# A chunk-selecting attention with a gated linear unit: one fp16 maximum for the bound's operands, and another order of the steps

## The chip, the cores and the metric

One core of one Trainium2 chip runs the whole program, one launch. Its TensorE (PE) multiplies, VectorE (DVE), ScalarE (ACT) and GpSimd (POOL) do the rest, and the queue of SyncE (SP) issues most transfers. The metric is the device time in microseconds of one execution.

## The reference

Batch 4, 8 heads, 768 positions, 64 dimensions, in float32. Keys are cut into 24 chunks of 32. For every query an upper bound of its score with each chunk is computed from the chunk's smallest and largest key values. The six causal chunks with the largest bounds are kept, and attention runs over these alone. Its output goes through a causal convolution of five taps, a sigmoid, a product with a value projection and an output projection.

```python
k_min, k_max = np.min(k_chunks, axis=3), np.max(k_chunks, axis=3)
ub = np.sum(np.maximum(q[:, :, :, None, :] * k_min[:, :, None, :, :],
                       q[:, :, :, None, :] * k_max[:, :, None, :, :]), axis=-1)
ub = np.where(causal, ub, -1000000000.0)
top_chunks = np.argsort(ub, axis=-1)[..., -6:]
scores = scale * np.matmul(q, k.transpose(0, 1, 3, 2))
scores = np.where(sel & causal_positions, scores, -1000000000.0)
attn = softmax(scores) @ v                       # then x = heads side by side, 512 wide
gate = 1.0 / (1.0 + np.exp(-causal_conv5(x, conv_w)))
return (gate * (x @ w_val)) @ w_out
```

## The kernel before

The work is 16 pairs of heads (four to a batch). A pair's two heads lie side by side on the 128 partitions. The kernel is a graph of named steps (`build`, inner function `pair`). They are emitted in an order written out by hand in `ORDER` (some 1,600 names), and each engine runs its own steps in that order. A step's name has the pair p behind it. Costs given with the steps (`cost`, `lat`, `dma`) are not used when the program is emitted.

- **Loads** `Lk`, `Lq`, `Lv`: keys, queries and values of a pair by SP's queue, into four buffers each. Pair 0 loads keys and queries in halves.
- **Transposes** `KT`, `QT` (PE, L649; L640 for pair 0) put keys and queries with the dimension on the partitions, in two PSUM banks of 384 columns each.
- **Evictions** `KE`, `QH` (ACT, L655, L692) write them as fp16; `QH` is 16 q.
- **Chunk extremes** `KX` (DVE, L661): four reductions a pair, maximum and minimum of two halves.
- **Bound operands.** With d = max - min, the bound is relu(q) d + q min. It is computed in fp16 with a high and a low part of each factor. `KB0` to `KB4` and `KS` (POOL, L671 to L688) make the parts of d and min. On DVE, from PSUM, for 640 of the 768 queries and in a 256 and a 384 wide piece: `QL` (L731) is the low part of q, `RH` (L746) relu of 16 q, `RL` (L753) the low part of the relu, as (q > 0) QL. For pair 2 `RH` is on ACT. Pair 0 goes another way: `KF`, `QF`, `RF` (ACT) make fp32 operands, and `BF` (PE, L723) multiplies in fp32.
- **Bounds** `CF` and `BD` (PE, L777, L788; six matmuls for each of five query tiles), **top eight** `T8` (DVE, L796), **compare** `CM` (DVE, L803) with the sixth largest. `MT` and `ME` (PE, then DVE, L817) transpose the mask; for six late pairs a transposing DMA `MD` does it.
- **Scores** `S` (PE, L831 to L836), in six PSUM banks per head: keys times queries, plus a penalty matmul of the mask (`EM`, `QM`). The 192 first query columns need no mask, so a piece that begins there is cut in two matmuls.
- **exp** `E` (ACT, L840; 12 a pair, ten of 512 columns), causal cut `A` on the diagonal (POOL, L852; 8 a pair), values as fp16 `VC` (POOL, L763).
- **Attention times values** `AV` (PE, L861), `RC` and `NR` (DVE) normalise, `XT`, `XTE` transpose (PE and DVE, L904; DMA for seven pairs), `XH` (POOL) copies what the convolution needs across tiles.
- **Convolution** `CV` (PE, L925; two halves of 80 matmuls for every second pair), `TH` (ACT) the gate as a tanh; **value projection** `VL` (PE, L940), `GV` (DVE, L946) gate times value; **output** `OU` (PE, L954), `OE` eviction (ACT, three on DVE), `ST` store (SP).
- **Spare matmuls** `F`, `G` (PE, L972): 36 matmuls whose result nobody reads.

PSUM has eight banks; a step that opens a group takes the bank that has been free longest. Weights (`wval`, `wout`) are loaded by POOL's queue, `wvd` copies a half of them by SP's.

Of the kernel before, what the change touches and what calls it, by code (L numbers as in the profile page):

```python
# [28 lines left out]
class Graph:
# [44 lines left out]
def emit_in_order(graph, names, nbanks=8):  # L74

    at = {o.name: o for o in graph.ops}
    order = [at[n] for n in names]
# [19 lines left out]
    "dmat": set(range(8, 15)),
    "dmam": set(range(10, 16)),
    "xeng": "DVE",
    "cvcost": 1750.0,  # L100
    "split": {0},
    "lq": {},
    "fine": {0},
    "vceng": "POOL",
    "f32": {0},
    "rha": {2},
    "rqeng": "ACT",
# [1012 lines left out]
```

## Time and profile before

| | us |
|---|---|
| runs | 188.33, 189.61, 313.72 (median 189.61) |
| span of the profiled execution | 185.7 |
| PE, DVE, ACT, POOL busy | 173.7, 133.2, 141.9, 103.6 |

The profile is of one execution, from its first to its last instruction; its own run time is not among the data, and the runs above lie 2.6 us and more over its span. A row of a group gives line, engine, operation, what is written and read, the shape and the count; then the busy time, the mean duration in ns, and the idle time of the engine just before, with what ended it. A row of the chain gives start, length and what ran. A step is found by its line.

### The profile page before, as it was taken

What the parts mean: (1) busy time and instruction counts of PE and PEld (TensorE: products, weight loads), DVE (VectorE), ACT (ScalarE), POOL (GpSimd) and SP (SyncE); (2) the same over time, 40 slices, a digit from 0 to 9 for tenths busy, and PEclk for the clock granted to TensorE, in tenths of its full rate; (3) what the DMA queues carried; (4) which work ended last, traced back from release to release, by engine and by line L of the source; (5) the groups of instructions that cost most, each with busy time, mean ns of one, the idle gap of its engine ahead of it and who ended that gap; (6) DMA issues with size and microseconds to landing.
All of it is one profiled execution on the core that took longest, in us unless ns stands there. A gap on an engine that the chain in (4) does not pass through costs nothing.

```text
span 185.7 us, 9267 instructions
## 1 busy us (share of the span) xinstructions
PE 173.7 (94%) x3894; PEld 120.0 (65%) x3894; DVE 133.2 (72%) x457; ACT 141.9 (76%) x322; POOL 103.6 (56%) x294
## 2 busy tenths in 40 slices
PE   7798889999999699999999899999999999999991
PEld 5685657675767576776767678675576646765550
DVE  0588899999999999999998798789425222710541
ACT  2656999999999789999898976837766999162341
POOL 8628789979295997589945408805850363100000
PEclk9999999999999999999999999999999999999999
DMA  4999999999999996099955748919938920017346
GB/s 104 212 220 195 220 178 234 200 196 185 213 176 227 210 195 88 4 203 201 197 106 124 158 91 164 115 35 230 241 101 219 209 95 4 13 38 287 115 167 229
DMA packets 89913, 29.70 MB, mean 160 GB/s; under 512 B 85387, under 2 KB 86667, under 8 KB 89872
## 3 DMA queue, kind: packets, MB, share of 16 engines
q1 hardware_dynamic: 88880, 28.06, 72.0%
q0 software_dynamic: 992, 1.06, 3.9%
q8 instruction: 30, 0.49, 1.1%
q14 instruction: 11, 0.09, 0.2%
HBM read 20.98 MB, written 6.29 MB: 147 GB/s over the span
## 4 chain that ended last, share of the span: by engine, by line
PE 64%; ACT 14%; POOL 6%; DVE 6%; issue 3%; DMA 2%; SPq 2%; DVEq 0%; POOLq 0%; ACTq 0%
PE ps L940 12%; PE ps L954 11%; ACT P L840 11%; PE ps L861 8%; PE ps L925 8%; PE ps L833 6%; PE ps L836 5%; PE ps L649 5%; PE ps L788 4%; DMA kn<-in_k_dram 2%; DVE KK L661 2%; POOL P L852 2%; POOL VA L763 2%; SPq L631 2%; ACT QH L692 1%
## 5 line engine op out<-in xcount | busy, mean ns | idle before, releaser
L840 ACT ACTIVATE P<-ps 128x512 f16<-128x512 f32 (+1 forms) x192 | 90.6, 574 | 7.7 <-PE ps L836 7.3
L852 POOL TENSOR_SCALAR_AFFINE_SELECT P<-P 128x128 f16<-128x128 f16 (+1 forms) x128 | 42.4, 356 | 24.0 <-ACT P L840 22.5
L661 DVE TENSOR_REDUCE KK<-ps 128x12 f32<-128x384 f32 x64 | 32.7, 549 | 8.7 <-PE ps L640 4.2
L836 PE MATMUL ps<-QM,EM 64*128 64x512 f16 (+4 forms) x256 | 37.5, 290 | 0.6 <-DVE QM L817 0.6
L833 PE MATMUL ps<-QH,KE 64*128 64x512 f16 (+4 forms) x256 | 35.4, 291 | 1.5 <-issue 0.8
L946 DVE SCALAR_TENSOR_TENSOR GV<-G,ps 128x384 f16<-128x384 f32 x32 | 16.4, 549 | 23.0 <-PE ps L940 23.0
L861 PE MATMUL ps<-VA,P 128*128 128x65 f16 x672 | 28.9, 194 | 0.0
L861 PEld LDWEIGHTS <-P 128*128 128x128 f16 x672 | 24.1, 98 | 6.5 <-issue 4.3
L962 ACT ACTIVATE OSB<-ps 128x512 f32<-128x512 f32 (+1 forms) x22 | 12.9, 603 | 16.1 <-PE ps L954 10.2
L940 PE MATMUL ps<-xT,wv 64*128 64x384 f16 x256 | 23.2, 323 | 0.0
L954 PE MATMUL ps<-wo,GV 128*128 128x512 f16 (+1 forms) x100 | 22.7, 371 | 0.0
L655 ACT ACTIVATE KE<-ps 128x384 f16<-128x384 f32 x32 | 15.7, 515 | 6.6 <-DVE KK L661 6.1
L796 DVE MAX8 TOP<-ps 128x8 f32<-128x16 f32 (+4 forms) x160 | 15.7, 166 | 4.3 <-PE ps L788 3.9
L930 ACT ACTIVATE G<-ps 128x384 f32<-128x384 f32 x32 | 13.8, 498 | 6.3 <-PE ps L925 6.3
L833 PEld LDWEIGHTS <-KE 64*128 64x128 f16 x256 | 13.6, 94 | 7.6 <-issue 3.3
L940 PEld LDWEIGHTS <-wv 64*128 64x128 f16 x256 | 12.9, 94 | 8.4 <-issue 1.4
L925 PE MATMUL ps<-xT,diag 32*32 32x384 f16 x1280 | 17.6, 326 | 0.0
L871 DVE TENSOR_TENSOR ON<-ps,RCP 128x384 f16<-128x384 f32 x32 | 17.1, 548 | 0.2
L692 ACT ACTIVATE QH<-ps 128x384 f16<-128x384 f32 x32 | 15.1, 507 | 2.1 <-PE ps L649 1.9
L925 PEld LDWEIGHTS <-diag 32*32 32x32 f16 x1280 | 14.1, 88 | 4.0 <-issue 1.6
L763 POOL CAST VA<-vn 128x768 f16<-128x768 f32 x16 | 14.3, 892 | 2.1 <-DMA vn<-in_v_dram 1.8
L836 PEld LDWEIGHTS <-EM 64*128 64x128 f16 x256 | 12.0, 94 | 4.9 <-issue 3.3
(80 smaller groups left out, 302.1 us busy)
## 6 DMA issues: line engine op xcount, KB each, us to landing
vn<-in_v_dram SPq DMA_DIRECT2D x16, 384.0 KB, 5.4
out_dram<-OSB SPq DMA_DIRECT2D x23, 256.0 KB, 2.9
kn<-in_k_dram SPq DMA_DIRECT2D x30, 192.0 KB, 4.5
qn<-in_q_dram SPq DMA_DIRECT2D x30, 192.0 KB, 4.5
wo<-in_moe_w_out_dram POOLq DMA_DIRECT2D x4, 128.0 KB, 3.8
wv<-in_moe_w_val_dram POOLq DMA_DIRECT2D x8, 64.0 KB, 3.3
wv<-wv SPq DMA_DIRECT2D x4, 128.0 KB, 5.0
kn<-in_k_dram SPq DMA_DIRECT2D x4, 96.0 KB, 2.4
```

The source lines that it names most:

```text
L661: nc.vector.tensor_reduce(out=KK[p % 2][:, mx, w * 12:(w + 1) * 12], in_=bank(gr, None).rearrange("p (c t) -> p c t", t=CH), axis=AX.X, op ...
L692: nc.scalar.activation(out=QH[p % 3][:, w * HB:(w + 1) * HB], in_=bank(gr, None), func=AF.Copy, scale=QS)
L763: nc.gpsimd.tensor_copy(out=o, in_=i)
L833: nc.tensor.matmul(out=pq[hh][:, col + a:col + n], lhsT=KE[p % 3][HP[hh], ks], rhs=QH[p % 3][HP[hh], q0 + a:q0 + n], start=True, stop=False)
L836: nc.tensor.matmul(out=pq[hh][:, col + a:col + n], lhsT=EM[HP[hh], ks], rhs=qm[HP[hh], q0 + a - 128:q0 + n - 128], start=False, stop=True)
L840: e.EX = lambda p, hh, bi, tot, gr: nc.scalar.activation(out=PT[hh, bi, p % 2][:, 0:tot], in_=bank(gr, None)[:, 0:tot], func=AF.Exp, scale ...
L852: nc.gpsimd.affine_select(out=ap, in_=ap, pattern=[[0, n], [1, 128]], compare_op=ALU.is_ge, fill=0.0, base=0, channel_multiplier=-1)
L861: nc.tensor.matmul(out=pav[:, qt, :], lhsT=PT[a, bi, p % 2][:, col:col + 128], rhs=VA[p % 3][:, hh, jt, :], start=(jt == 0), stop=(jt == qt))
L871: e.NR = lambda p, hh, gr: nc.vector.tensor_tensor(out=ON[(p // 2) % 2][:, 2 * (p % 2) + hh].rearrange("p t h d -> p h t d"), in0=bank(gr, ...
L925: nc.tensor.matmul(out=pc[i][os], lhsT=diag[rs, cp * NG + gi, j, :], rhs=x[rs, gi, :, a:a + 128], start=(j == 0), stop=(j == 2 * KSZ - 1), ...
L940: nc.tensor.matmul(out=pv[h], lhsT=wval_sb[HP[h], n, wc:wc + 255:2], rhs=xT[HP[h], (b % 2) * 2 + cp, gi, :, LD:LD + 128], start=(n == 0), ...
L954: nc.tensor.matmul(out=po[:, 0:z - a], lhsT=GVT[(b % 2) * NCT + et][:, s * 128:(s + 1) * 128], rhs=wout_sb[:, et, a:z], start=(et == 0), s ...
```

## The change

- `RH` and `RL` are replaced by one step `RR`: maximum with 0 of the high and the low part of q together, 2 x 640 columns of fp16 from SBUF to SBUF, on DVE. For that `QL` lies beside `QH` in one tile, and `QH` is rounded down a little in its scale (16 (1 - 2^-11)), so that the low part has the sign of q.
- Pair 0 goes the fp16 way like the others, and its loads are whole. `KF`, `QF`, `RF`, `BF` go.
- The parts of d and min are made in six steps `KB0` to `KB5` without an intermediate tile.
- An unmasked piece of the scores is no longer cut in two matmuls; 64 matmuls fewer, the same columns.
- The table `alt` gives 71 steps another engine than the usual one: to DVE 14 `KE`, 13 `QH`, 19 `OE`, 14 `KB`, two `XH` and one `VC`; to ACT five `ME`, two `XTE`, one `KB`.
- 43 spare matmuls in five groups.
- `ORDER` is another order of the steps, with the PSUM bank of each group written behind an @.

```diff
 PARAMS = {
-    "kbeng": ["POOL", "POOL", "POOL"],
     "border": [5, 3, 4, 2, 1, 0],
...
+    "alt": dict(w.split(":") for w in """
+KB0.1:ACT ME0:ACT KE2.1:DVE KE3.0:DVE QH4.0:DVE XTE0:ACT ME3:ACT KE5.1:DVE QH5.1:DVE ME4:ACT
+QH6.0:DVE KB6.2:DVE KB6.5:DVE KE7.0:DVE QH7.1:DVE KE8.0:DVE KB7.5:DVE QH8.1:DVE KB7.2:DVE
...
+OE3.5z:DVE OE3.5:DVE OE3.0:DVE OE3.3:DVE OE3.2:DVE OE3.1:DVE
...
 ORDER = """
+mfz em0 em1 ident mKB0 Lk0 F0@2 F1 F2 F3 F4 F5 F6 F7 F8 F9 F10 F11 F12 F13 KT0@01 KX0.11 KX0.00
+cfill mNS0 identh ident2 identb KE0.1 mVA2 mKB1 Lq0 em2 KX0.10 Lk1 G0@4 G1 G2 G3 G4 G5 G6 G7 G8 G9
+G10 QT0@23 H0@1 H1 H2 H3 H4 H5 H6 H7 H8 H9 H10 KT1@45 KX0.01 Lq1 QH0.0 Lk2 Lq2 Lk3 Lq3 QL0.0 QH0.1
+KB0.0 KB0.1 KB0.2 KE0.0 KE1.0 KB0.3 Lv0 Lk4 KB0.5 QL0.1 KB0.4 mVA0 RR0 KX1.10 KX1.11 CF0@6 CF1@7
...
-QS = 16.0
+QR = 16.0
+QS = QR * (1.0 - 2.0 ** -11)
...
-            g.op(eng, cr, lr, f"RH{p}.{w}", lambda w=w, gr=gr, eng=eng: e.RHv(p, w, gr, eng),
-                 [("Q", "ps", p, w)], [("RH", k2, w)], [gr])
...
-            g.op("DVE", c, l, f"RL{p}.{w}", lambda w=w, gr=gr: e.RLv(p, w, gr),
-                 [("Q", "ps", p, w), ("QL", k2, w)], [("RL", k2, w)], [gr])
...
+        eop("DVE", f"RR{p}", lambda eng: e.RRv(p, eng),
+            [("QH", k3, w) for w in range(2)] + [("QL", k3, w) for w in range(2)], [("RR", k2)])
...
-    RH = [ct_([128, SELT * 128], F16, f"RH{i}") for i in range(2)]
-    RL = [ct_([128, SELT * 128], F16, f"RL{i}") for i in range(2)]
+    QQ = [ct_([128, 2, S], F16, f"QQ{i}") for i in range(3)]
+    QH = [t[:, 0] for t in QQ]
+    RR = [ct_([128, 2, SELT * 128], F16, f"RR{i}") for i in range(2)]
...
+    def scaled(eng, out, in_, f):
+        if eng == "ACT":
+            nc.scalar.activation(out=out, in_=in_, func=AF.Copy, scale=f)
+        elif f == 1.0:
+            (nc.vector if eng == "DVE" else nc.gpsimd).tensor_copy(out=out, in_=in_)
+        else:
+            (nc.vector if eng == "DVE" else nc.gpsimd).tensor_scalar(
+                out=out, in0=in_, scalar1=f, scalar2=None, op0=ALU.mult)
...
+        hh = n % 2
+        o, i = kb[HP[hh], :, CC[hh] * NCH:(CC[hh] + 1) * NCH], kk[HP[hh]]
+        if n < 4:
+            scaled(eng, o[:, 0:2], i, 1.0)
         else:
...
+            en.tensor_tensor(out=o[:, 2:4], in0=i, in1=o[:, 0:2], op=ALU.subtract)
...
+    def RRv(p, eng):
+        (nc.vector if eng == "DVE" else nc.gpsimd).tensor_scalar(
+            out=RR[p % 2], in0=QQ[p % 3][:, :, 128:S], scalar1=0.0, scalar2=None, op0=ALU.max)
...
-                if a:
-                    nc.tensor.matmul(out=pq[hh][:, col:col + a], lhsT=KE[p % 3][HP[hh], ks],
-                                     rhs=QH[p % 3][HP[hh], q0:q0 + a], start=True, stop=True)
-                nc.tensor.matmul(out=pq[hh][:, col + a:col + n], lhsT=KE[p % 3][HP[hh], ks],
-                                 rhs=QH[p % 3][HP[hh], q0 + a:q0 + n], start=True, stop=False)
+                nc.tensor.matmul(out=pq[hh][:, col:col + n], lhsT=KE[p % 3][HP[hh], ks],
+                                 rhs=QH[p % 3][HP[hh], q0:q0 + n], start=True, stop=False,
+                                 skip_group_check=True)
```

Up to the step `CV3.0` the two orders hold the following numbers of steps on DVE and ACT (before, after). DVE: `KX` 52, 52; `RH` 22, 0; `RL` 24, 0; `QL` 24, 26; `RR` 0, 12; `KE` 0, 9; `QH` 0, 8; `ME` 10, 5; `XTE` 8, 6; `KB` 0, 5; `T8` 60, 60; `NR` 19, 19. ACT: `E` 132, 128; `KE` 26, 17; `QH` 28, 18; `ME` 0, 5; `XTE` 0, 2; `TH` 8, 8.

More of the change, by code (lines that the diff above doesn't have):

```diff
@@ L66, in op, with emit_in_order @@
         o.preds = list(preds)
-        o.succs = []
-        for q in o.preds:
-            self.ops[q].succs.append(o.idx)
         self.ops.append(o)
         return o
-def emit_in_order(graph, names, nbanks=8):
+def emit_in_order(graph, words, nbanks=8):
     at = {o.name: o for o in graph.ops}
-    order = [at[n] for n in names]
-    assert len(at) == len(graph.ops) == len(order) == len(set(names))
-    free = list(range(nbanks))
+    order = [w.partition("@")[::2] for w in words]
+    assert len(at) == len(graph.ops) == len(order) == len({n for n, _ in order})
+    free = set(range(nbanks))
     done = set()
-    for o in order:
-        assert all(q in done for q in o.preds), o.name
+    for name, banks in order:
+        o = at[name]
+        assert all(q in done for q in o.preds), name
         done.add(o.idx)
-        for g in o.groups:
-            if g.bank is None:
-                g.bank = free.pop(0)
+        new = [g for g in o.groups if g.bank is None]
+        assert len(new) == len(banks), name
+        for g, b in zip(new, banks):
+            g.bank = int(b)
+            free.remove(g.bank)
         o.emit()
@@ L90, in emit_in_order @@
             if g.left == 0:
-                free.append(g.bank)
+                free.add(g.bank)
 PARAMS = {
-    "kbeng": ["POOL", "POOL", "POOL"],
     "border": [5, 3, 4, 2, 1, 0],
[L97 to L107, printed above, removed]
+    "xtdma": set([8, 9, 10, 11, 12, 13, 14]),
+    "mtdma": set([10, 11, 12, 13, 14, 15]),
@@ L613, with load @@
     cq = {"k": (kn, k), "q": (qn, q), "v": (vn, v)}
-    def load(what, p, part, nsp, eng):
-        en = nc.sync if eng == "SP" else nc.scalar
+    def load(what, p):
         t, src = cq[what]
@@ L718, in BF @@
-    def BF(p, it, gr):
-        pu = bounds(gr)
-        ts = slice((it - 1) * 128, it * 128)
-        CF(it, pu)
-        for n in range(2):
-            nc.tensor.matmul(out=pu[:, it - 1, :], lhsT=QF[:, 1 - n, ts],
-                             rhs=KF[:, n, :], start=False, stop=(n == 1))
-    e.BF = BF
+            return
+        if n == 1:
+            scaled(eng, kk, kk, KS)
+            return
+        hh = n % 2
+        o, i = kb[HP[hh], :, CC[hh] * NCH:(CC[hh] + 1) * NCH], kk[HP[hh]]
```

675 lines of the change are left out of this document (252 added, 423 removed).

## Prediction

> **What bounds the kernel now.** I read the head of the page, then the busy time in five stretches, then the chain that ended last. The stretches are cut at the first exp (17.9 us) and at the start of CV3.0 (99.2 us), a step that stands at the same amount of attention work in both orders.
>
> ```profile
> PE 173.7 (94%) x3894; PEld 120.0 (65%) x3894; DVE 133.2 (72%) x457; ACT 141.9 (76%) x322; POOL 103.6 (56%) x294
> ```
> ```profile
> 0.00:17.90 17.90, 14.64 (x146) 12.00 (x148) 10.25 (x39) 9.20 (x23) 11.55 (x29) 1.00 0.93 184
> 17.90:50.00 32.10, 30.34 (x609) 20.57 (x606) 31.16 (x120) 31.25 (x73) 25.26 (x72) 1.00 1.03 201
> 50.00:67.00 17.00, 14.93 (x433) 11.63 (x430) 16.06 (x48) 15.15 (x38) 13.65 (x40) 1.00 1.06 209
> 67.00:99.20 32.20, 31.53 (x764) 22.53 (x761) 30.68 (x117) 30.89 (x72) 23.60 (x67) 1.00 0.73 132
> 99.20:182.00 82.80, 82.24 (x1960) 53.28 (x1959) 44.41 (x136) 55.42 (x123) 29.52 (x89) 1.00 0.61 138
> ```
>
> The columns are length, then PE, weight load, DVE, ACT, POOL busy (with counts), granted clock, DMA share, GB/s. The clock is 1.00 throughout. PE at 94% looks like the bound, but its busy time counts overlapping latencies, so I weigh its work by runs without gaps:
>
> ```profile
> 78.76 0.76 PE ps L788 x30
> 119.67 1.30 PE ps L940 x16
> 157.50 2.76 PE ps L861 x84
> 161.99 2.03 PE ps L925 x160
> 175.76 6.17 PE ps L954 x32
> 181.96 0.69 DVE OSB L964
> ```
>
> A value projection group (VL, L940) costs 1.30 us, a convolution (CV, L925) 2.03, an output tile (OU, four L954; two of these eight are half wide) 0.77, an attention-value matmul (L861) 33 ns, one of the bound (BD, L788) 25 ns. All of OU (20 us), sixteen groups of VL (20.8) and twelve half CVs (12) lie behind the cut at 99.2; with the scores, bounds and AV left there I count 78 us of matmul in 82.8. So behind the cut PE is the bound. Ahead of it the same count gives 73 us in 99, while DVE and ACT are filled: from 17.9 to 99.2 DVE is busy 77.9 of 81.3 us (31.16 + 16.06 + 30.68) and ACT 77.3. **The kernel is two stages:** a DVE and ACT stage of 81 us behind a head of 18, and a PE stage of 83. After 182.0 only the last eviction and its store follow.
>
> **The change, part by part.** First the price of one instruction in a full queue.
>
> ```profile
> 23.30 0.94 DVE KK L661 x2
> 45.44 3.80 ACT P L840 x8
> 84.03 0.76 ACT KE L655 x2
> ```
> ```profile
> L746 DVE TENSOR_SCALAR RH<-ps 128x384 f16<-128x384 f32 x14 | 7.7, 549 | 1.3 <-ACT QH L692 0.8 <-PE ps L649 0.5
> L753 DVE SCALAR_TENSOR_TENSOR RL<-ps,QL 128x384 f16<-128x384 f32 x15 | 8.2, 545 | 0.0
> L753 DVE SCALAR_TENSOR_TENSOR RL<-ps,QL 128x256 f16<-128x256 f32 x15 | 6.1, 413 | 0.1
> L904 DVE COPY xT<-ps 128x768 f16<-128x768 f16 x9 | 4.9, 552 | 2.5 <-PE ps L893 2.5
> L817 DVE COPY QM<-ps 128x640 f16<-128x640 f16 x10 | 4.8, 477 | 0.0
> L710 ACT ACTIVATE QF<-ps 128x384 f32<-128x384 f32 x2 | 1.0, 494 | 0.0
> L710 ACT ACTIVATE QF<-ps 128x256 f32<-128x256 f32 x2 | 0.7, 408 | 0.0
> L698 ACT ACTIVATE KF<-KK 64x24 f32<-64x24 f32 x4 | 0.7, 213 | 0.0
> L744 ACT ACTIVATE RH<-ps 128x384 f16<-128x384 f32 x1 | 0.5, 485 | 0.0
> L744 ACT ACTIVATE RH<-ps 128x256 f16<-128x256 f32 x1 | 0.4, 390 | 0.0
> ```
>
> On DVE 384 columns last 549 ns but take 0.465 us of the queue (0.93 for two), so 0.085 of every duration lies under the next. The 256-column form takes 413 - 85, 0.33. On ACT an eviction of 384 columns takes 0.38, an exp 0.475, hence some 0.57 for 640 and 0.67 for 768.
>
> *RH and RL go, RR comes.* Ahead of the cut 22 RH and 24 RL leave DVE, half of each width: 46 x 0.40 = 18.4 us. Twelve RR come: 1,280 columns of fp16 from SBUF to SBUF, which no row shows. The two fp16 copies from PSUM differ by 75 ns for 128 columns, 0.59 ns a column. At that rate RR takes 0.39 + 0.38 = 0.77; at twice that rate 0.39; at the fp32 rate of the rows above (132 ns for 128) 1.4. I take 0.6, nearest to the fp16 rows and somewhat under their rate, since RR has no PSUM side: 12 x 0.6 = 7.2. [...]
>
> *RR as a wait.* RR needs both halves of QL, where RH needed only the transposed q; but QL stands just ahead of it on DVE, and BD needed QL already. The q banks come free two DVE instructions earlier. I count neither.
>
> *Evictions change engines.* Ahead of the cut nine KE and eight QH go to DVE, 17 x 0.465 = +7.9 us, and five ME (-2.0) and two XTE (-0.9) leave it. Two QL for pair 0 (+0.8), five small KB steps (some 0.1 each by T8's row further down, +0.5) and the coarser CM of pair 0 (-0.3) remain. DVE in all: -18.4 + 7.2 + 7.9 - 2.0 - 0.9 + 0.8 + 0.5 - 0.3 = **-5.2 us**. ACT loses 9 KE and 10 QH (-7.2), gains five ME and two XTE (+4.2), has four exps fewer ahead of the cut (-1.5), and loses the fp32 forms of pair 0 (KF, QF, RF) and two RH, 3.3 by the last five rows: **-7.8**. DVE remains the later of the two.
>
> *POOL* keeps its load: six KB steps a pair as before, now for sixteen pairs, the same VC and A. It was busy 62.5 us of 81.3. A KB step on DVE waits for POOL's step before it, and DVE's queue stands behind it; that costs between nothing and one POOL instruction (0.41 for an A, row below), five times ahead of the cut, at most 2 us, kept for the range.
>
> *The head.* These rows show it before:
>
> ```profile
> 0.80 2.04 SPq L631 DMA_DIRECT2D kn<-in_k_dram  x4
> 5.39 1.16 DVE L661 TENSOR_REDUCE KK<-ps 128x12 f32<-128x384 f32 x2 [4.22 <-PE ps L640]
> 17.92 3.05 ACT L840 ACTIVATE P<-ps 128x512 f16<-128x512 f32 x6
> ```
> ```profile
> kn<-in_k_dram SPq DMA_DIRECT2D x30, 192.0 KB, 4.5
> L723 PE MATMUL ps<-KF,QF 128*128 128x48 f32 x20 | 2.8, 281 | 0.0
> L683 POOL COPY KB<-KC 64x96 f16<-64x96 f16 x30 | 7.7, 261 | 1.4
> L803 DVE TENSOR_TENSOR NS<-ps,TOP 128x240 f16<-128x240 f32 x15 | 6.0, 397 | 0.6 <-DVE TOP L796 0.5
> 21.55 0.83 DVE TOP L796 x10
> 16.19 0.44 PE L813 MATMUL ps<-identh,NS 128*128 128x128 f16 x5
> ```
>
> Before, pair 0 goes in halves of 96 KB, its bounds in fp32 matmuls, and DVE does the reductions of pairs 2 and 1 in between. Now two whole transfers issue at 0.8 and 1.3, and at 4.5 us to landing KT0 starts near 5.8, its reductions near 6.4, a microsecond later than before. Then: four reductions (8.3); six KB steps of 0.26 (9.9), under which QL and RR are done; BD, 30 matmuls, 0.76 (10.7); T8 0.83 and CM 0.4 (11.9); MT 0.44, ME on ACT 0.57, first scores 0.4 by estimate (13.4). Hand-overs between engines and Lk1 behind Lq0 make it worse; I take 14.5, and as bounds 13.4 and 17.9. That is **-3.4 us**, and holds some 1.2 of DVE's 5.2.
>
> *Matmuls.* The unsplit scores drop 64 of the narrow matmuls, with the same columns. Seven more spare matmuls lie in waits of the head. BF's 2.8 us goes with pair 0. Behind the cut PE has the same list: nothing. Nineteen output evictions and ten KE/QH go to DVE there, 44 to some 58 us of 83, with PE still the bound.
>
> *Loads and banks.* Four issues fewer on SP; order and four-deep buffers stay. The PSUM bank of each step is written out where it was the first free one; there are eight in both. Nothing.
>
> **Sum.** Head -3.4; the rest of stage one -4.0 at DVE's share of 0.96, -4.2; stage two 0. The span goes from 185.7 to 178.1. The runs shown (188.33 and 189.61; 313.72 is an outlier) lie 2.6 and 3.9 above the profiled span, whose own run time isn't given. With 3.2 between, I predict **181.3 us** against a median of 189.61. A difference of 2% (3.8 us) is about what a measurement here can tell from none.
>
> **Rivals.**
>
> *More than the sum.* The stretch from 50 to 67 is ragged, and the chain there runs through POOL:
>
> ```profile
> 60.32 0.91 POOL VA L763
> 62.46 0.87 POOL VA L763
> ```
> ```profile
> POOL P L852 <- ACT P L840: 22.5, 18, 8.8
> L852 POOL TENSOR_SCALAR_AFFINE_SELECT P<-P 128x256 f16<-128x256 f16 x64 | 25.8, 414 | 13.5 <-ACT P L840 12.6
> ```
>
> POOL sat idle 22.5 us behind ACT's exps, then had VC and KB steps in one pile, and PE lost 2 of 17 us. An order without that pile, with ACT's -7.8 and the low end for RR, gives the 2 us back and 2.5 by RR, another 4 to 5 in all: 176 to 179. For it: both filled engines get lighter. Against: DVE is refilled on purpose to balance. Chance 0.2.
>
> *RR and POOL shut each other out.* All large DVE rows ahead of the cut read PSUM, RR alone works in SBUF on both sides, as POOL does. If RR must wait for the POOL instruction under way, it waits up to 0.41 (an A) or 0.91 (VC, rows above): 12 x 0.41 = 4.9 to 12 x 0.91 = 10.9 us on DVE, hence 186 to 192. [...] POOL is busy 77% of stage one, but a wait is on average half an instruction, some 2 us in all, which still lies within the forecast's own stretch. Chance 0.18, with a stage two that stalls for DVE's added 14 us, which would give the same times.
>
> *Slower than before: POOL's queue becomes the bound.* Place: pairs 3 to 9. POOL works in order, A waits for an exp, and the next pair's KB steps, hence its bounds, masks and scores, stand behind it. Price: in the stretch from 50 to 67 ACT stood still for 1.9 of 17 us. With such a pile at each of eight pairs it is 15 us, 181 + 15 = 196; from six or seven piles on it decides. For: POOL's load is the same while the others' falls, 62.5 us against some 74. Against: fourteen KB steps move to DVE. 0.07.
>
> *The change does not do what it says:* the two orders are equally good and the relief runs into exps waiting for scores; only the head shows, 186. 0.05.
>
> **Chances.** Forecast (179 to 186) 0.5. The line of 2% lies at 185.8. Faster: the forecast, the first rival and, since the second and fourth begin at 186, a sixth of these two (0.04): 0.74. Same: the rest of the two, 0.19. Slower than 193.4: 0.07. Low end 176.5 (low ends of RR and of the head, no pile), high end 188.
>
> **What will show it.** RR's row: 0.4 to 0.8 us, and POOL rows that last longer beside it if they exclude each other. First exp at 13.5 to 15.5. CV3.0 near 91.6, with DVE still at 0.95 of the stretch ahead of it. From CV3.0 to the last eviction 82 to 83 us. It is wrong if stage two grows (PE stalls behind GV or OE on DVE), or if DVE idles ahead of CV3.0.

## The result, and the profile after

The changed kernel took 190.78 us (median of four runs, 190.06 to 191.33), the kernel before 188.97 in the same comparison: ratio 1.0117, interval 1.0068 to 1.0166. It is 1.2% slower, inside the bound of 2%. The forecast was 181.3 with a range up to 188. Ratios, here and below, compare each kernel's runs within 1.5% of its fastest, while medians take all of its runs.

First the head of the page and the busy times between the same marks (first exp, start of CV3.0, last matmul) of the changed kernel; columns as before.

```profile
PE 172.5 (92%) x3855; PEld 121.3 (64%) x3855; DVE 144.4 (77%) x467; ACT 124.0 (66%) x277; POOL 100.7 (53%) x280
```
```profile
0.00:16.10 16.10, 13.57 (x150) 9.52 (x152) 7.87 (x27) 6.07 (x12) 8.69 (x27) 1.00 1.09 190
16.10:97.40 81.30, 75.94 (x1770) 55.47 (x1766) 75.10 (x273) 74.48 (x168) 64.72 (x176) 0.98 0.80 160
97.40:184.10 86.70, 83.02 (x1945) 56.35 (x1942) 61.41 (x169) 42.85 (x97) 27.25 (x77) 1.00 0.74 148
```

The first exp comes 1.8 us earlier (17.9, now 16.1). Stage one lasts 81.3 us in both, although DVE and ACT each work 2.8 us less in it (77.9 to 75.10, 77.29 to 74.48). Stage two grows from 82.8 to 86.7, the tail by 0.5. That is -1.8 + 0 + 3.9 + 0.5 = +2.6, the difference of the spans (185.7, 188.3). The granted clock, 1.00 throughout before, is 0.98 in stage one.

The chain of the changed kernel (share of the span by engine), and four of its pieces in order of time (start, length):

```profile
PE 46%; POOL 21%; DMA 13%; DVE 9%; issue 4%; ACT 2%; SPq 1%; POOLq 0%; DVEq 0%
```
```profile
107.72 6.45 DMA wo<-in_moe_w_out_dram
126.32 5.59 DMA vn<-in_v_dram
146.39 3.53 DMA QM<-NS
155.75 5.52 DMA xT<-ON
```

Before, the chain was PE 64%, ACT 14%, POOL 6%, DMA 2%. Now stage two, where PE was to be the bound, has these four transfers in its chain, 21.1 us together. Added up from the rows of the chain, stage one has 30.8 us of POOL where it had 11.8, and 1.1 of ACT where it had 26.1. The queue of SP shows why transfers are late (waits of the changed kernel: total, times, longest):

```profile
SPq L644 <- DVE NS L628: 18.6, 3, 9.1
SPq L861 <- DMA wv<-in_moe_w_val_dram: 12.0, 1, 12.0
```

wvd0 (L861) holds the queue for 12 us from 65 us on, and MD10 (L644) for nine more until 88.8: nothing is issued from it between 65.3 and 77.4 us, nor between 79.6 and 88.8. Eight loads and three copies of weights then go out between 90 and 108 us. The last columns but one, the DMA share, of the kernel before and of the changed one:

```profile
80.00:88.00 8.00, 7.98 (x180) 5.74 (x177) 7.51 (x38) 7.81 (x19) 7.40 (x23) 1.00 1.19 209
88.00:108.00 20.00, 18.87 (x622) 14.09 (x618) 17.61 (x60) 18.26 (x45) 11.39 (x33) 1.00 0.67 136
```
```profile
80.00:88.00 8.00, 7.37 (x168) 5.71 (x167) 7.38 (x28) 7.48 (x16) 7.33 (x23) 1.00 0.22 49
88.00:108.00 20.00, 18.08 (x563) 13.02 (x561) 15.27 (x48) 14.17 (x33) 10.04 (x27) 1.00 0.96 169
```

What went at 209 GB/s up to 88 us now crowds the 20 us behind it, at a share of 0.96.

### The profile page after: what moved, and what is told of

It is laid out like the page before. It is cut to its first block, busy times and chain, and to the rows that moved or that the text cites. A ratio compares the mean times of both kernels' runs of the same rounds, so it can differ in the third digit from the quotient of the medians.

```text
span 188.3 us, 9145 instructions
## 1 busy us (share of the span) xinstructions
PE 172.5 (92%) x3855; PEld 121.3 (64%) x3855; DVE 144.4 (77%) x467; ACT 124.0 (66%) x277; POOL 100.7 (53%) x280
## 3 DMA queue, kind: packets, MB, share of 16 engines
q1 hardware_dynamic: 88816, 28.06, 73.9%
## 4 chain that ended last, share of the span: by engine, by line
PE 46%; POOL 21%; DMA 13%; DVE 9%; issue 4%; ACT 2%; SPq 1%; POOLq 0%; DVEq 0%
PE ps L774 8%; PE ps L685 8%; POOL P L676 7%; PE ps L745 6%; PE ps L614 5%; PE ps L760 5%; PE ps L655 4%; PE ps L522 4%; DMA wo<-in_moe_w_out_dram 3%; PE ps L659 3%; DMA vn<-in_v_dram 3%; DMA xT<-ON 3%; POOL VA L531 3%; POOL KB L562 2%; DMA kn<-in_k_dram 2%
## 5 line engine op out<-in xcount | busy, mean ns | idle before, releaser
L676 POOL TENSOR_SCALAR_AFFINE_SELECT P<-P 128x128 f16<-128x128 f16 (+1 forms) x128 | 43.8, 367 | 31.5 <-ACT P L664 19.2
L655 PE MATMUL ps<-QQ,KE 64*128 64x512 f16 (+3 forms) x256 | 37.2, 308 | 0.3 <-ACT P L664 0.3
L745 PE MATMUL ps<-xT,diag 32*32 32x384 f16 x1280 | 18.7, 326 | 1.8 <-POOL xT L531 0.9
L622 DVE MAX8 TOP<-ps 128x8 f32<-128x20 f32 (+4 forms) x160 | 16.4, 167 | 4.1 <-PE ps L614 4.0
L760 PEld LDWEIGHTS <-wv 64*128 64x128 f16 x256 | 14.2, 94 | 7.5 <-issue 1.8
L655 PEld LDWEIGHTS <-KE 64*128 64x128 f16 x256 | 14.5, 96 | 5.6 <-issue 1.1
L659 PEld LDWEIGHTS <-EM 64*128 64x128 f16 x256 | 14.0, 95 | 6.1 <-issue 3.8
L745 PEld LDWEIGHTS <-diag 32*32 32x32 f16 x1280 | 14.2, 88 | 6.0 <-issue 2.7
L529 ACT ACTIVATE OSB<-ps 128x512 f32<-128x512 f32 x6 | 3.6, 598 | 21.5 <-PE ps L774 21.5
L614 PE MATMUL ps<-KB,RR 128*128 128x48 f16 x240 | 15.5, 185 | 1.7 <-POOL KB L562 1.4
L574 DVE SCALAR_TENSOR_TENSOR QQ<-ps,QQ 128x256 f16<-128x256 f32 (+1 forms) x32 | 14.5, 481 | 1.7 <-ACT QQ L529 1.6
```

The lines of the kernel that those rows point to most:

```text
L614: nc.tensor.matmul(out=o, lhsT=lt, rhs=KB[i2][:, j, :], start=False, stop=(n == 5), skip_group_check=True)
L655: nc.tensor.matmul(out=pq[hh][:, col:col + n], lhsT=KE[p % 3][HP[hh], ks], rhs=QH[p % 3][HP[hh], q0:q0 + n], start=True, stop=False, skip_ ...
L659: nc.tensor.matmul(out=pq[hh][:, col + a:col + n], lhsT=EM[HP[hh], ks], rhs=qm[HP[hh], q0 + a - 128:q0 + n - 128], start=False, stop=True, ...
L676: nc.gpsimd.affine_select(out=ap, in_=ap, pattern=[[0, n], [1, 128]], compare_op=ALU.is_ge, fill=0.0, base=0, channel_multiplier=-1)
L745: nc.tensor.matmul(out=pc[i][os], lhsT=diag[rs, cp * NG + gi, j, :], rhs=x[rs, gi, :, a:a + 128], start=(j == 0), stop=(j == 2 * KSZ - 1), ...
L760: nc.tensor.matmul(out=pv[h], lhsT=wval_sb[HP[h], n, wc:wc + 255:2], rhs=xT[HP[h], (b % 2) * 2 + cp, gi, :, LD:LD + 128], start=(n == 0), ...
```

## The experiments

Stage lengths are measured between the marks above, in the profiled run of each kernel. The profiled runs of e9, e11, e15 and e17 lie 0.8, 1.8, 0.4 and 1.2 us above their medians. e2, e4 and e8 have one run each, e12 and e14 two. The kernel before was measured anew beside each group, with medians of 189.2 to 190.1. The edits are shown in short, by the names of the steps.

| kernel | first exp | stage one | stage two | PE, DVE, ACT, POOL busy in stage one | median us |
|---|---|---|---|---|---|
| before | 17.9 | 81.3 | 82.8 | 76.8, 77.9, 77.3, 62.5 | 188.97 |
| changed | 16.1 | 81.3 | 86.7 | 75.9, 75.1, 74.5, 64.7 | 190.78 |
| e3_rr_alone | 18.7 | 82.7 | 82.9 | 78.6, 67.8, 77.1, 63.9 | 189.75 |
| e6_rr_act | 19.2 | 84.7 | 82.9 | 77.8, 71.2, 74.2, 63.5 | 192.34 |
| e7_rr_act2 | 17.3 | 88.3 | 83.1 | 78.7, 75.2, 71.2, 65.3 | 193.99 |
| e12_act_less | 19.4 | 84.9 | 83.2 | 78.8, 67.1, 71.0, 63.5 | 192.75 |
| e13_pe_less | 18.8 | 82.4 | 83.5 | 74.8, 67.5, 76.4, 64.2 | 190.28 |
| e14_both_less | 17.5 | 85.8 | 83.2 | 73.9, 66.8, 70.7, 65.1 | 191.30 |
| e2_rr_twice | 14.3 | 85.2 | 86.5 | 77.7, 80.9, 75.7, 66.9 | 191.98 |
| e1_queues | 14.1 | 86.8 | 93.6 | 76.9, 76.1, 75.1, 67.2 | 199.66 |
| e4_no_cut | 15.8 | 80.7 | 84.0 | 75.1, 75.4, 74.6, 38.3 | 186.65 |
| e5_handoffs | 14.2 | 79.7 | 87.1 | 74.6, 74.1, 74.6, 65.1 | 187.23 |
| e8_no_gh | 15.0 | 89.2 | 85.1 | 79.6, 75.1, 74.4, 64.3 | 195.25 |
| e9_queues2 | 15.7 | 84.8 | 83.1 | 76.2, 74.3, 74.8, 67.4 | 188.50 |
| e10_cwl | 15.9 | 79.5 | 87.5 | 75.0, 75.7, 74.3, 63.8 | 188.53 |
| e11_cwt | 15.7 | 84.5 | 85.8 | 76.5, 74.6, 74.9, 67.2 | 189.92 |
| e15_queues3 | 15.9 | 79.4 | 87.5 | 74.8, 74.2, 74.4, 67.1 | 188.18 |
| e16_loads_up | 15.7 | 78.6 | 85.7 | 74.7, 74.1, 73.8, 65.0 | 185.88 |
| e17_all_up | 15.8 | 79.8 | 86.0 | 75.4, 74.3, 73.7, 66.9 | 186.11 |

### Does less work make stage one shorter?

**e3_rr_alone**, in the kernel before:

```diff
-RH{p}.0 RH{p}.1 RL{p}.0 RL{p}.1        (p = 1 to 15)
+RR{p}                                  (in the place of the last RL)
```

> The kernel before with one part of the change alone: RR, one fp16 maximum for each pair but the first, stands in the place of the last RL of the pair, and RH and RL go; the order, the tiles' engines, the spare matmuls and the eight matmuls of pair 0 stay as before. It takes per pair two maxima of 640 columns on ACT or VectorE and two on VectorE away for one on VectorE. Theory, VectorE bounds stage one of the kernel before, so that work taken from it is time taken from the stage: stage one falls by 4 to 6 us, the time to 183 to 185. Rival, the order bounds it (each engine waits where its list makes it wait): stage one falls by 0 to 2 us, the time is 187 to 189.

Ratio to before 1.004 (0.9987 to 1.0093): nothing. DVE lost 10.1 us of stage one and the stage did not shrink. Its profiled run has one stretch of 3.41 us at half the clock in that stage (from 65.0), the one of before has none. In the stretch of the changed kernel (23.6 to 27.0 us) a matmul of the bound starts 40 ns after the last, elsewhere 25. As an estimate from the granted 0.50, a stretch costs at most half its length, here 1.7 us, and 82.7 less 1.7 is 81.0. The waits of DVE in stage one, before and in e3_rr_alone (first rows of each):

```profile
DVE NS L803 <- DVE TOP L796: 0.5, 1, 0.5
DVE RCP L867 <- PE ps L861: 0.5, 2, 0.3
```
```profile
DVE KK L655 <- PE ps L643: 2.5, 3, 1.7
DVE RCP L847 <- PE ps L841: 2.3, 5, 0.9
DVE QQ L725 <- ACT QQ L686: 2.1, 3, 1.1
DVE TOP L776 <- PE ps L768: 1.9, 3, 0.9
```

What the engine no longer works, it waits: for transposed keys, for AV, for ACT's QH, for the bound. Being busy for 96% of a stage it had not been its bound.

**e2_rr_twice**, in the changed kernel:

```diff
+        for _ in range(2):
             nc.vector.tensor_scalar(out=RR[p % 2], ...)
```

> The changed kernel with each fp16 maximum (RR) issued twice into the same buffer, so that VectorE carries 16 more of them, 0.48 to 0.6 us each: some 5 us more in stage one (about 11 pairs), 2.5 us more in stage two. Theory, VectorE bounds stage one still: stage one goes from 81.3 to 86 or more, the time to 195 to 197. Rival, VectorE has slack in stage one and it is the chain between engines that lasts 81 us: stage one grows by 2 us or less, the time is 191 to 194.

Stage one 85.2, so 3.9 us of the added 5.8 show, nearly as the theory had it. The time, 191.98 in the single run, lies where the rival had it, since the head was 1.8 us shorter. Work added to DVE costs time here (3.9 us for 5.8) and work taken from it brings none (0 for 10.1 in e3_rr_alone). Neither theory had both. A reading that fits, not shown: a step that others wait for is late at once, and early only as far as everything ahead of it is.

**e6_rr_act, e7_rr_act2**, on top of e3_rr_alone:

```diff
-KE{p}.1 on ACT                          (p = 2 to 11)
+KE{p}.1 on DVE
 e7 only:
-QH{p}.1 on ACT                          (p = 2 to 11)
+QH{p}.1 on DVE
```

> RR alone in the kernel before (as in e3_rr_alone), and ten copies KE p.1 (p = 2 to 11) go from ACT to VectorE at their old place of the order: ACT loses 10 x 0.53 us in stage one, VectorE, which had 14 us of waits there in e3_rr_alone, gets 5.5 us. Theory, ACT is the engine that bounds stage one of the kernel before (4 us idle in it, 6 us in e3_rr_alone), which is why RR alone gave nothing: stage one falls from 82.7 to 78 to 80, the time to 184.5 to 187. Rival, the order and the banks that a step has to wait for bound it, no single engine: stage one falls by less than 1 us, the time is 189 to 190.

> As e6_rr_act, and ten copies QH p.1 (p = 2 to 11) go from ACT to VectorE too: ACT loses some 10.5 us of stage one against e3_rr_alone, VectorE gets 11, about what RR had taken from it. Theory, ACT bounds: stage one falls to 75 to 78 us, unless VectorE is full again by then (then 78 to 80 as in e6_rr_act); the time is 182 to 186. Rival, order and banks bound it: no gain over e3_rr_alone, 189 to 190, or a loss, since QL then waits for a QH on its own engine.

Slower: ratios 1.0271 (1.0185 to 1.0358) and 1.0343 (1.0266 to 1.042). ACT works 3 and 6 us less, DVE 3.4 and 7.4 more, still below what it did before, and the stage grows by 2.0 and 5.6. So less work on ACT alone doesn't shorten the stage either; that the moved copies arrive later on DVE is the likely reason. In e6_rr_act exp waits 7.0 us for scores (2.3 before, 4.2 in e3_rr_alone):

```profile
ACT P L828 <- PE ps L824: 7.0, 13, 1.6
```

**e12_act_less, e13_pe_less, e14_both_less** take work away and give it to nobody:

```diff
 e12 and e14:
-KE{p}.0 KE{p}.1                         (p = 3 to 11)
 e13 and e14:
-for hh in range(2):                     # the mask's matmuls of a score block
+for hh in range(0 if 3 <= p <= 11 else 2):
```

> e3_rr_alone (the kernel before with RR alone) with the 18 copies KE p.0 and KE p.1 of pairs 3 to 11 left out, so that these pairs use the keys of pairs 0 to 2: ACT loses some 9.5 us of the 77.1 that it works in stage one, and no other engine gets work. Theory, ACT bounds stage one, and e6 and e7 failed because VectorE hands the keys over late: stage one falls from 82.7 to 74 to 77 us, the time to 181 to 184. Rival, no single engine bounds it (TensorE, ACT and VectorE hand the work on in one order): stage one falls by 2 us or less, the time is 187 to 189.

> e3_rr_alone with the mask's matmuls (the second product of each score block) left out for pairs 3 to 11: TensorE loses about as many columns as the scores' first product has there, some 8 to 9 us of the 17.7 that lie between the starts of these matmuls in stage one. Theory, TensorE bounds stage one (it is busy 78.6 of its 82.7 us in the records of e3_rr_alone): stage one falls by 5 to 9 us, the time to 181 to 185. Rival, it waits for the exponentials anyway: by 2 us or less, 187 to 189.

> What e12_act_less and e13_pe_less leave out, together. If one of the two engines alone bounds stage one, this gains no more than that one run of the two; if the two bound it together, each run alone gains little and this one 6 to 10 us (stage one 73 to 77); if it is the order of the hand-overs with VectorE and POOL, 3 us or less here too.

Stage one of e14_both_less:

```profile
17.50:103.30 85.80, 73.89 (x1663) 53.64 (x1660) 66.79 (x250) 70.74 (x159) 65.07 (x178) 0.96 0.90 167
```

PE 2.9, DVE 11.1 and ACT 6.6 us below before, and the stage is 4.5 us longer. Ratios 1.0182 (1.0091 to 1.0273), 1.0013 (0.9958 to 1.0068) and 1.0106 (1.0009 to 1.0203). Part of the loss is the clock: two stretches at half the clock in stage one of e12_act_less and of e14_both_less, one in that of e13_pe_less. With 1.7 us taken off for each, the stages are 81.5, 82.4 and 80.7, against 81.3 before. So the rival held in what it said of the stage, though the times lie above its range: with the order fixed, stage one does not follow the work of DVE, ACT or PE, nor, in the changed kernel, of POOL (e4_no_cut, next). What is left is the chain of hand-overs between them; that is a conclusion by exclusion.

**e4_no_cut**, in the changed kernel:

```diff
-            lambda hh=hh, bi=bi: e.AS(p, hh, bi), [keys[hh]],
+            lambda: None, [keys[hh]],
```

> The changed kernel with the 128 causal cuts on POOL left out (so the triangle of each diagonal block isn't zeroed): POOL loses 43.8 us of work, some 26 of them in stage one. Theory, POOL's list is what holds stage one at 81.3 us (POOL has 21% of the chain): stage one falls by 4 us or more. Rival, POOL only shows up in the chain because its entries wait for others: stage one falls by less than 1.5 us, and stage two by what AV waits for POOL there, 1 us or less.

One run, 186.65. Without 26 us of POOL's work stage one is 0.6 us shorter. Stage two loses 2.7 of its 3.9, more than the rival's 1: POOL is busy there for only 27 of 87 us, but its copies, casts and loads stand in line behind the cuts.

### Which waits are new?

**e5_handoffs and e10_cwl**, in the changed kernel:

```diff
 ORDER:   ... KB0.4 mVA0
+cwl
 RR0 ... KB1.4
-cwl
 e5 only, in alt:
-KB6.2:DVE KB6.5:DVE KB7.5:DVE KB7.2:DVE KB11.0:DVE
```

> The changed kernel with two hand-offs between engines taken out of stage one: the load cwl goes up to a place ahead of RR0 (so that POOL, and behind it TensorE's cwt, no longer wait for it at 18 to 23 us), and KB6.2, KB6.5, KB7.2, KB7.5 and KB11.0 go from VectorE back to POOL (so that POOL no longer waits for VectorE in the middle of a pair's key bounds, 3.8 us at 59 to 62.7). Theory, new waits on POOL in stage one use up what VectorE and ACT gained: TensorE's waits for POOL of 1.1 to 1.2 us each go, stage one falls from 81.3 to 78.5 to 79.5, the time to about 188. Rival, the waits only move: stage one changes by less than 1 us, the time stays at 190 to 191.

> The changed kernel with one of the two hand-offs of e5_handoffs alone: cwl goes up ahead of RR0; the five KB steps stay on VectorE. Theory, the wait at 22 us is what counts, since the granted clock falls to 0.50 for 3.4 us right behind it in the changed kernel (23.6 to 27.0): the clock is 1.00 in every run, the time 188 to 189, some two thirds of the gain of e5_handoffs. Rival, the KB steps count (POOL waits 3.8 us for them at 59 us): the time stays at 190 to 191.

e5_handoffs: ratio to before 0.9908 (0.9853 to 0.9962), against 1.0117 of the changed kernel, which is 2% from moving one 10 KB load and putting back five small steps. e10_cwl: 188.53, ratio 0.9949 (0.989 to 1.0007), clock at least 0.998 in all ten runs, as its theory had it. So the load alone is most of it, and in stage one all of it: 79.5 us here, 79.7 in e5_handoffs, though POOL still waits 3.5 us for KB6.2 here. The changed kernel around it (matmuls in order of time; then busy times and clock):

```profile
21.84 0.29 PE L659 MATMUL ps<-QM,EM 64*128 64x256 f16 x2
23.21 0.73 PE L875 MATMUL ps<-ident,cwn 5*128 5x5 f32 x8 [1.09 <-POOL cwn L851]
```
```profile
22.10:23.60 1.50, 0.41 (x8) 0.39 (x7) 1.42 (x4) 1.48 (x4) 1.39 (x3) 1.00 1.06 218
23.60:27.00 3.40, 3.40 (x60) 2.85 (x58) 1.86 (x6) 1.88 (x6) 3.13 (x10) 0.50 0.79 170
```

PE waits 1.09 us for the copied taps of the convolution, whose load went out at 17.42 and landed at 21.15, and pays a second time: from 23.6 to 27.0 the granted clock is 0.50. In e5_handoffs its longest wait there is 0.67, and the clock keeps 1.00.

**e11_cwt**, on top of e9_queues2 (below):

```diff
-cwt@7 QT3@10 RR2 cws KX3.11 QH3.0 S1.3@52
+QT3@10 RR2 KX3.11 QH3.0 S1.3@52 cwt@7 cws
```

> e9_queues2 with cwt and cws five steps later, behind S1.3, so that TensorE does not stand 0.67 us at 22.0 waiting for VectorE's copies of the taps (cwT). Theory, waits of TensorE in stage one add up: stage one falls by 0.3 to 0.7 us against e9_queues2, the time by as much. Rival, what TensorE gains there it waits for the exponentials' banks later: no change, or up to 0.5 us slower since the diagonals come later.

Ratio to before 0.9945 (0.986 to 1.003) against 0.9961 of e9_queues2, its median 189.92 against 188.50: the rival held, no gain to be seen from taking the last 0.67 us away.

### Where did stage two's four microseconds come from?

**e1_queues**, in the changed kernel:

```diff
-wvd0 wvd3 wvd1 wvd2   at their places from 65 us on
+wvd0 wvd3 wvd1 wvd2 CV3.0
+wval31 wout2 wout3 wout1 wout0
+Lv12 Lv13 XT8
+NR13.0 XT13 NR12.0 XT12
-XH13:DVE
```

> The changed kernel with a few steps of the order moved, none of its arithmetic: the four wvd steps (which make the queue of SP wait for the value weights) go from stage one to just ahead of CV3.0, the loads of wo go up behind wval31, the loads Lv12 and Lv13 and the transposes XT12 and XT13 go up by up to a few places, and XH13 goes back to POOL. Theory, late transfers: the 3.9 us by which stage two grew (86.7 after, 82.8 before) are waits of TensorE for transfers that stand in order behind a blocked entry of a queue. Then stage two falls to about 83 to 84 us, stage one stays at 81.3 and the time is about 187. Rival, the order of TensorE's steps itself: stage two stays at 86 to 87 and the time at 190 to 191.

199.66 us, ratio 1.0552 (1.0449 to 1.0656): far from both, with stage one at 86.8 and stage two at 93.6. What stood in SP's queue behind an entry that waited went out after it. With wvd0 gone MD10 stood there for 19.0 us, until 87.4, and XT13, moved up with XT12 behind it, for 11.9 us until its normalised values were there (the first two rows are waits, that of L708 between 100 and 165 us; then two issues):

```profile
SPq L643 <- DVE NS L627: 19.0, 1, 19.0
SPq L708 <- DVE ON L694: 11.9, 1, 11.9
150.75 3.57 SPq L708 DMA_TRANSPOSE xT<-ON  x2
154.38 2.59 SPq L643 DMA_TRANSPOSE QM<-NS  x2
```

The masks MD14 and MD15 (154.38) came late behind these, and PE stood for 6.96 us from 151.4 on. Too many moves in one kernel; the next ones were smaller.

**e9_queues2 and e15_queues3**, on top of e5_handoffs:

```diff
 both:
+Lv12 Lv13 XT8
+XT13 XT12
 e9:
+wval31 wout0 wout1 wout3 wout2
 e15:
+wout0 wout1 wout3 VC9 ... A9.13 wout2
```

> e5_handoffs with seven steps of its queues moved up and nothing else: the four loads of wo (POOL's queue) go to just behind wval31, in the stretch of 75 to 90 us where the DMA engines stand half idle; Lv12 and Lv13 (SP's queue) go ahead of XT8 and XT9; XT12 goes to just behind XT13, ahead of four stores. Theory, late transfers make stage two 4 us longer (its idle time of TensorE is 4.3 us in e5_handoffs against 0.5 before, and 2.4 of that end with the landing of wo, or with XH11 and the conv behind Lv12, or with NR14.0 behind XH13): stage two falls from 87.1 to 84.5 to 85.5 us, the time from 187.2 to 185 to 186. Rival, the steps only wait for the next thing: stage two stays above 86.3 and the time at 187.

> e5_handoffs with the transfers of e9_queues2 moved up, but the four loads of wo at places where POOL stands idle in e5_handoffs: three ahead of VC9 (POOL waits 1.7 us there for the values of pair 9), the fourth behind A9.13. Theory, stage two loses its late transfers as in e9_queues2 (83.1 there) and stage one stays at 79.7, since POOL's cuts are not pushed back: the time is 184 to 186. Rival, what TensorE is freed of in stage two it waits for elsewhere, as in e9_queues2: 187 to 188.5.

e9: stage two fell to 83.1, as expected of late transfers, and stage one rose by 5.1. Ratio 0.9961 (0.9916 to 1.0007), no better than e5_handoffs. Four transfers issued on POOL took 2.11 us of its queue at 85.9, and Lv9, issued 1.0 us later than in e5_handoffs, took 8.5 us to land instead of 4.2 (95.8 instead of 90.5). Its cast and three cuts came behind it, and AV waited 2.98 us until 98.07; the trace leaves open whether that wait was for them (below). e15: 188.18, the rival's number, and 0.9878 (0.9826 to 0.9929), the same as e5_handoffs within the intervals. PE waited for POOL's steps in stage one as long as in e5_handoffs, 2.1 us, but this stood in stage two (matmuls of e15_queues3):

```profile
96.53 0.33 PE L655 MATMUL ps<-QQ,KE 64*128 64x384 f16 x2
100.65 0.42 PE L659 MATMUL ps<-QM,EM 64*128 64x384 f16 x2 [3.79 <-issue]
```

"issue" means that no semaphore ended the wait, and the trace gives the matmul at 100.65 none at all. Counting PE's instructions, weight loads and matmuls, in order of time from 0, the first one behind the wait is number 4033, which is 15 x 256 + 193. In the traces of all nineteen kernels there are 46 idle stretches over 0.15 us of this kind after 20 us, and all 46 end at a number 193 beyond a multiple of 256: 1985, 2241, 3521, 3777, 4033 or 4289. The page has 30 packets in a queue of instructions:

```profile
q8 instruction: 30, 0.49, 1.1%
```

They are of 16,384 bytes each, and 30 for PE's 7,766 instructions is one for every 259: about one for each block of 256. The page counts their time as a share of the same 16 DMA engines as that of the loads (1.1% beside 73.9% for q1 in the changed kernel). The traces hold the start of each packet too. Set side by side in order, PE's number 256 k + 193 never begins sooner than 2.2 us after the start of packet k, in any of the nineteen traces, and the 46 stretches end 2.2 to 3.2 us after that start (4.0 for the longest). The packet for 4033 started when PE still had 172 instructions to go in the changed kernel and 211 in e16_loads_up (below). In e15_queues3 it started at 96.61, when PE had none left. By these starts the stretches are waits of PE for its own instructions, and the long one a packet that started late. AV's wait in e9_queues2 stands at such a place as well, number 3777: its packet started at 95.03, when PE had reached it, 3.04 us before PE went on, and POOL's last cut ended 0.18 us before. Either may have ended it.

**e16_loads_up and e17_all_up**, on top of e5_handoffs:

```diff
 both:
+Lv9 Lk13 Lq13 Lv10 MD10
+Lv12 Lv13 XT8
 e17 only:
+wout0 wout1 wout3 VC9 ... A9.13 wout2
+KB10.4 VC8
```

> e5_handoffs with six loads earlier in the queue of SP and nothing else: Lv9, Lk13, Lq13 and Lv10 go ahead of MD10, where SP stands waiting from 75 to 85 us with the DMA engines half idle, and Lv12 and Lv13 ahead of XT8. In every trace so far the idle times of TensorE that no semaphore ends begin at its instruction number 193 of a block of 256 (two of them at 96.4 and 101.5 us in e5_handoffs, 1.04 and 0.67 us; 3.79 in e15_queues3), as if the next block of instructions, a packet of 16384 bytes on the same DMA engines, came late in the crowded stretch from 86 to 105 us. Theory, it is that: with 1.5 MB of loads out of that stretch the two idle times shrink to under 0.6 us together, that of 0.92 behind Lv12 goes, stage two falls from 87.1 to 84.5 to 85.5 and the time to 185 to 186. Rival, the fetch has nothing to do with the loads: idle times at the same two numbers as before, 186.5 to 187.5.

> e16_loads_up with the loads of wo at the idle places of POOL as in e15_queues3, and VC8 behind KB10.4 (so that BD of pair 10 doesn't wait 0.9 us for POOL). Theory, with the loads out of the way the transfers of wo no longer hold up TensorE's instructions, and the wait of 1.06 us for wo goes too: 184 to 185.5. Rival, four more transfers in that stretch bring back a late block of instructions as in e15_queues3 (3.79 us): 187 to 189.

e16: 185.88, ratio 0.9829 (0.9769 to 0.9889), as its theory had it; stage two, 85.7, is just above the theory's range. The same place of the list in the changed kernel (two idle stretches without a semaphore) and in e16_loads_up (one is left; the other is down to 0.14):

```profile
99.97 0.34 PE L659 MATMUL ps<-QM,EM 64*128 64x384 f16 x2 [1.05 <-issue]
...
104.75 0.50 PE L760 MATMUL ps<-xT,wv 64*128 64x384 f16 x4 [0.39 <-issue]
```
```profile
96.15 0.34 PE L658 MATMUL ps<-QM,EM 64*128 64x384 f16 x2 [0.35 <-issue]
```

In e17, with four more transfers there, 1.13 and 0.74 us are back at numbers 4033 and 4289, while the wait for wo (1.50 in e16) is gone; 186.11, ratio 0.9816 (0.9754 to 0.9879), no different from e16 and between theory and rival. That the transfers beside it are what delays a packet is inferred from the stretches growing and shrinking with them; no view shows a packet waiting.

**e16 is 1.7% faster than the kernel before and some 2.8% faster than the changed one** (0.9829 / 1.0117), with all of the change's arithmetic, and no work moved between engines except the five KB steps put back. Against e5_handoffs the intervals overlap.

### The head

**e8_no_gh**, in the changed kernel:

```diff
-G0@4 G1 ... G10
-H0@1 H1 ... H10
```

> The changed kernel without 22 of its 43 spare matmuls, the two blocks of 11 between the first transposes of keys and of queries. In the profile of the changed kernel these took 2.46 and 1.5 us and the first queries, landed at 7.0 us, were transposed at 8.7; in other profiles of the same list they took 1.3 us each, since TensorE's rate had doubled earlier (109 ns instead of 213 for 256 columns). Theory, they only delay: the first exponential starts at 13.5 to 14.5, up to 2 us earlier than at 16.1. Rival, they are what brings the doubled rate: without them the small matmuls up to the first exponential run at the low rate, first exponential at 14.5 to 17.

One run, 195.25. First exp at 15.0, 1.1 us earlier than in the changed kernel and 0.9 later than in e1, where they ran at the high rate. The spare matmuls that are left start some 0.2 us apart until 12.07 and 0.12 at 12.98, so the rival's low rate held. But 195.25 us is 4.5 slower. PE idled 2.14 us ahead of the taps at 20.9, and 2.30 and 2.23 us ahead of late blocks of instructions at 59.7 and 95.0; behind each the clock was 0.50, from 22.4 to 29.3, from 63.4 and from 97.5. Neither theory counted that, and one run can't say how much of it is due to the 22 matmuls.

## Why the prediction was wrong, step by step

The span was forecast at 178.1 us and is 188.3. Of these 10.2 us, 1.6 lie in the head, 4.2 in stage one, 3.9 in stage two and 0.5 behind the last matmul.

- **Head, -3.4 (first exp 14.5): the term was right for one of two cases.** 16.1 in the changed kernel; in kernels with the same head 14.1, 14.2 and 14.3 (e1, e5, e2) or 15.7 to 15.9 (e4, e9, e10, e11, e15, e16, e17). The difference is when PE doubles its rate (matmuls of the changed kernel, then of e5_handoffs):

```profile
6.20 2.53 PE L788 MATMUL ps<-fz 128*128 128x256 f16 x11
8.66 0.90 PE L522 MATMUL ps<-ident,qn 64*128 64x64 f32 x12
```
```profile
5.60 1.38 PE L788 MATMUL ps<-fz 128*128 128x256 f16 x11
7.07 0.59 PE L522 MATMUL ps<-ident,qn 64*128 64x64 f32 x12
```

  The same eleven spare matmuls take 2.53 or 1.38 us (some 213 or 109 ns each), with 1.00 in the clock column both times. The prediction's durations for the head came from later rows, at the high rate. Which of the two cases a traced execution got is luck, by the last section.

- **Stage one, -4.2: this step failed.** Its busy terms were near. DVE was to lose 5.2 and lost 5.2 (10.25 + 77.9 to 7.87 + 75.10), ACT 7.8 and lost 5.9 (9.20 + 77.29 to 6.07 + 74.48). What failed is "at DVE's share of 0.96": that a stage shrinks with the busy time of its fullest engine. e3 took 10.1 us from DVE and gained nothing; e12 to e14 took from ACT and PE too. Some of the 4.2 was there behind one hand-over: with cwl moved up stage one is 79.4 to 79.7 (e5, e10, e15), about what the half clock behind PE's wait had cost, and with the loads of e16 78.6. The prediction's fourth rival said so ("the relief runs into exps waiting for scores; only the head shows", 186) and had 0.05. Its own test named both signs, a DVE that idles ahead of CV3.0 (in stage one 5.1 us of it end with another engine, 2.2 before) and a stage two that grows. The first could have been seen: PE, DVE and ACT were all within 5 us of filling the stage, so relief of one had at most the slack of the others, and nothing said that even this was to be had in a fixed order.

- **RR at 0.6, and RR beside POOL: right, and of no weight.**

```profile
L581 DVE TENSOR_SCALAR RR<-QQ x16: 477/492/2199, 11.1 to 139.9; 128x1280 f16<-128x1280 f16 x16
```
```profile
138.60 0.93 POOL L531 CAST VA<-vn 128x768 f16<-128x768 f32 x1
139.41 1.02 POOL L531 COPY xT<-xT 128x32 f16<-128x32 f16 x2
140.50 0.30 POOL L676 TENSOR_SCALAR_AFFINE_SELECT P<-P 128x128 f16<-128x128 f16 x1
```

  (Shortest, middle and longest RR in ns; then POOL at the end of the longest.) In nine of the sixteen no POOL instruction runs at RR's start, or one that ends within 0.15 us: RR takes 0.48 to 0.49 us. In four of these the next step on DVE starts 0.40 us after RR does, near the low end of 0.39; what RR gains by having no PSUM side no run shows apart. In the other seven RR ends 0.34 to 0.44 us after the end of a POOL instruction that overlaps it: six last 0.55 to 0.96 us, and the one of pair 15 lasts 2.20 us, from 137.76 to 139.96, over four cuts and VC, which ends at 139.52. POOL's two copies at 139.41 take 1.02 us, the five other pairs of them 0.46 to 0.48. These ends fit the rival in which the two shut each other out. The twelve RR ahead of CV3.0 take 0.61 us on average. What they take beyond 0.48 is 1.6 us of DVE, not the rival's 4.9 to 10.9, over all sixteen 3.3, and only 0.1 us of PE's idle time in stage two ends with an RR.

- **Five KB steps on DVE, "at most 2 us": right, and beside the one that was missed.** POOL waited 3.8 us for KB6.2, but e10, which keeps these steps on DVE, has the stage one of e5 without them. What cost time was cwl, and the prediction named it nowhere.

- **Stage two, 0: failed, but not where it was looked for.** It said the stage would be wrong if PE stalled behind GV or OE on DVE. DVE went from 44.4 to 61.4 us in it, and 0.6 us of PE's idle time ends with DVE there. The failing step is "Loads and banks ... Nothing": the new places of wvd0, MD10 and wout held the queues until 88 us, and then data, masks and instructions came late together. With the transfers moved up stage two was 83.1 in e9. PE's idle stretches over 60 ns in stage two (no matmul and no weight load on record) add up to 3.6 us against 0.5 before, 3.1 of the stage's 3.9. Of these 3.6, 1.4 end without a semaphore, 0.4 with wo, 0.4 with a mask, and 1.3 with POOL's and DVE's steps for the convolution; that these stood behind a late load and a late transpose fits e9, where POOL's is gone.

- **3.2 us from span to run: mis-sized.** It is 1.7 us in every run since. The rest was the clock of the kernel before. In the comparisons here, without two runs far off, its twelve runs at 1.00 have a median of 187.4 us, fifteen at 0.99 188.4, thirty-three at 0.98 189.4 and twenty-four at 0.97 190.9. The quoted execution of before (clock 1.00) was one of its quickest. The low end of 176.5 is not the sum of its terms either: 181.3 less 2.5 for RR, 1.1 for the head and 2 for the pile is 175.7.

- **POOL as the bound (0.07):** e4 speaks against it in stage one. The result lies slower than the forecast for another reason.

## What to carry to other kernels

In a program with a fixed order on each engine, busy 95% doesn't make an engine the bound (DVE was busy for 77.9 of 81.3 us, and 10.1 less left the stage as it was): take its work away on paper and ask what it would wait for next; if that is another engine as full, the order has to change, not the work. After any reordering, read the waits of the DMA queues first: here two entries that waited for 12.0 and 9.1 us held what stood behind them, and the transfers then came in one crowd, at a DMA share of 0.96, with masks, values and, by their packets, PE's own instructions among them. Repairs should be one step at a time, since e1 and e9 paid for each wait removed with a new one.

## What the chip showed that was not expected

- **Half the clock for 3.4 us at a time, on a fixed grid.** Every stretch of low granted clock inside the runs is 0.50 and lasts 3.4, 6.8 or 10.2 us. Most follow an idle time of PE: 1.09 us (changed kernel, 22.1), 2.14, 2.30 and 2.23 (e8), 2.08 and 6.96 (e1), 3.79 (e15). In the nineteen traces every idle time of 1.89 us and more has one that begins within it or just behind it, and of the shorter ones only some have: 1.51 us in e16 and 1.78 in e11 passed without, and one in the head of e3 has no such time ahead of it. So the length of the idle time alone does not decide. By the medians above (187.4 us at clock 1.00, 188.4 at 0.99) one such stretch costs the kernel before some 1.0 us, an estimate. Where a trace has several, counting the one that comes in each behind the last matmul, their starts lie whole multiples of 3.413 us apart, in all 23 cases (22.45, 63.41, 97.54 in e8: 12 and 10 times).
- **The doubling of PE's rate in the head falls on the same grid.** In the changed kernel four steps back from 23.63 is 9.98; spare matmuls start 0.21 us apart up to 9.89 and 0.11 apart from 10.05 on. In e5 the grid has 4.71, the last slow one is at 3.86 and a transpose at 5.08 is fast. In each of the nineteen traces a line of its grid lies between the last slow and the first fast ones. So the two heads, 14.2 and 16.1, come with where the grid lies in an execution; e5 and e10, with one list up to the first exp, have the one (14.2) and nearly the other (15.9).
- **PE waited at one place of a block of 256 of its instructions**, for up to 3.8 us where transfers crowd (e15), and in the kernel before for 0.78 and 0.48 (at 64 and 104 us); by the packets' starts the block came late.
- Open: which chain of hand-overs sets the 79 to 81 us of stage one. The runs show which engines' work does not. The PSUM banks, written out in the changed order, were not tried apart from it.
